# Row operands for the weight gradients: packed fp32 transposes in place of bf16 ones

## The chip, the cores and the metric

The kernel runs on one core of one Trainium2 chip. The metric is device time in microseconds of one execution. TensorE (PE) multiplies, VectorE (DVE) and ScalarE (ACT) work on tiles, GpSimd (POOL) does small copies and starts some of the DMA transfers, SyncE (SP) starts the others. Tiles lie in SBUF as 128 partitions by some number of elements; matmul results and transposes land in PSUM, of which the kernel uses eight banks of 128 x 512 fp32.

## The reference

Forward and backward of a speech encoder with a joint network, all tensors bf16. With B = 2, T = 16000, D = 256:

```
h  = gelu(conv(x, w1, 3 taps))[:, ::2]      # 8000 steps
f  = gelu(conv(h, w2, 3 taps))[:, ::2]      # 4000 steps
fe = f @ w_f;  ge = g @ w_g                 # ge: 8 rows
j  = tanh(fe[:, :, None] + ge[:, None])     # 4000 x 8
out = j @ w_o
# and, from grad_out (2, 4000, 8, 256), by the chain rule:
# the gradients of x, w1, w2, g, w_f, w_g and w_o
```

The gradients of w1, w2 and w_f are sums over time of outer products: for each tap, `dw[i] = sum over t of input[t + i]^T gradient[t]`. A matmul sums over partitions, so for these three gradients the inputs and gradients are needed with time in the partitions ("rows"), while all other work here holds the channels in the partitions.

## The kernel before

One unit of time is a quarter step q (4 steps of x, 2 of h, 1 of f). The 4000 steps of f of each batch are cut into 8 chunks of 512 (the last has 416), 16 chunks in all. Inside a chunk, `blocks` cuts 512 into four blocks of 128 steps (416 into 128, 128, 128, 32).

A chunk n goes through these stages, and each is a Python generator that yields after each small group of instructions:

- `conv_units`, `conv2_units`, `fe_units`: the forward pass (matmuls L241, L274, L297; gelu by helper L191), channels in partitions. Tile HT holds h as even and odd steps (`par` 0 and 1), FT holds f, G1 and G2 the gelu derivatives.
- `joint_units`, once per pair of the 8 rows u: matmul with w_o transposed (L518), the tanh derivative on DVE (L520), the output matmul (L574) and its copy on ACT (L576), the sum over u by an identity matmul (L531) into NGFE, and the gradient of w_o (`gwo`, L621), whose row operand JR is made by DMA transposes on SP's queue (L548).
- `d1_units`, `d5_units`: backward through w_f (L334, tile GF) and through w2 (L363, tile GH, even and odd steps). `d1_units` also issues the loads of x rows (`load_x5`): tile X5 holds, for each of 128 quarter steps, five steps of x in a row (4q-1 to 4q+3), 2560 bytes in one partition.
- `gw2_units`: the gradients of w2 and w_f. First it makes rows. For each block of 128 steps, eight 128x128 bf16 PE transposes (helper `transposes`, L374) go into one PSUM bank: HT even, HT odd, HT odd one step earlier, GF, each in two halves of 128 channels. One DVE copy of 128x1024 (L376) moves them to a tile of pool `rowp`. Then FT and NGFE are transposed, two blocks to a bank. Then come 8 matmuls of 256 columns for each of three taps (L416), and 8 for w_f (L425). Each sum stands in PSUM and is added by DVE to an fp32 accumulator in SBUF (`flush`, L317).
- `e_units`: transposes of GH (16 in two banks), the gradient of x (`gx_block`, L467, copied by ACT at L470, stored by POOL's queue at L479), and the gradient of w1 (`gw1`, L489, 16 matmuls of 256 columns per tap, rows of GH against X5).

So a chunk has 64 bf16 transposes and 8 copies L376 for these rows, and 80 matmuls of 256 columns that use them. Chunks of 511 or 417 steps arise in `e_units`, where the window of x is shifted by one step. The other transposes at L374, of JT, belong to `jr_block` and have no part in the change.

The order is written by the main loop: while chunk n's `joint_units` runs as `main`, `weave` takes units of a `fill` chain, in which the backward stages of chunk n-1 and the forward stages of chunk n+1 alternate (`islice(gw2, 6)` ends after the six groups of transposes, `islice(e, 5)` after two groups of transposes and three more units). The last chunk's backward stages run alone after the loop. Pools hand out tiles in a ring: `rowp` six, `x5p` four, PSUM `psp` five banks. A stage that asks for a tile of a ring waits until the last reader of the tile that it replaces is done.

POOL's queue carries, in order, the x row loads (L170, L173, L177), the stores of the x gradient (L479) and of the output (L605), and small copies. At the start POOL makes the identity and issues the loads of w1 (L642), g (L644) and w_g (L645).

Of the kernel before, what the change touches and what calls it, by code (L numbers as in the profile page):

```python
# [13 lines left out]
BF16 = mybir.dt.bfloat16  # L14
FP32 = mybir.dt.float32
# [6 lines left out]
P = 128  # L22
KT = 2
KK = 3
D = 256
# [6 lines left out]
def kernel(  # L32
# [22 lines left out]
    nc = tc.nc  # L55
    B, T, _ = x.shape
    MQ = T // 4
    NCH = (MQ + CW - 1) // CW
# [9 lines left out]
    def blocks(w):  # L68
        return [(o, min(P, w - o)) for o in range(0, w, P)]

    pool = lambda name, bufs, **kw: ctx.enter_context(tc.tile_pool(name=name, bufs=bufs, **kw))
    const = pool("const", 1)
    xcp = pool("xcp", 6)
# [6 lines left out]
    gfp = pool("gfp", 2)  # L80
    ghp = pool("ghp", 2)
    rowp = pool("rowp", 6)
    x5p = pool("x5p", 4)
    gxp = pool("gxp", 2)
    jtp = pool("jtp", 7)
    gotp = pool("gotp", 5)
# [10 lines left out]
    def ps_f32():  # L97
        return psp.tile([P, 512], FP32, name="ps", tag="ps")
# [3 lines left out]


    ident = const.tile([P, P], BF16, name="ident")
    W1 = const.tile([P, KK, KT, D], BF16, name="W1")
    W2 = const.tile([P, KK, KT, D], BF16, name="W2")
    WF = const.tile([P, KT, D], BF16, name="WF")
# [53 lines left out]
        return lo, hi  # L161

    def load_x5(n, o, M):
        pin = tc.keep_in_program_order
        b = chunks[n][0]
        q0 = window(n)[0] + o
        t = x5p.tile([P, 5, D], BF16, name="X5")
        if q0 == 0:
            nc.vector.memset(t[0:1, 0, :], 0.0)
            pin(nc.gpsimd.dma_start(out=t[0:1, 1:5, :], in_=x[b, 0:4, :].rearrange("(o f) d -> o f d", o=1)))  # L170
            src = x[b, 3:4, :]
            ap5 = bass.AP(tensor=src.tensor, offset=src.offset, ap=[[4 * D, M - 1], [1, 5 * D]])
            pin(nc.gpsimd.dma_start(out=t[1:M].rearrange("p f d -> p (f d)"), in_=ap5))  # L173
        else:
            src = x[b, 4 * q0 - 1:4 * q0, :]
            ap5 = bass.AP(tensor=src.tensor, offset=src.offset, ap=[[4 * D, M], [1, 5 * D]])
            pin(nc.gpsimd.dma_start(out=t[:M].rearrange("p f d -> p (f d)"), in_=ap5))  # L177
        S[n]["X5", o] = t

    def scratch(name, spare):  # L180
# [138 lines left out]
    def d1_units(n):  # L319
        b, ci, c0, W = geom(n)  # L320
        st = S[n]
        lo, hi = window(n)
        for (o, M) in blocks(hi - lo):
# [46 lines left out]
    def transposes(srcs, dsts):  # L370

        ps = ps_bf()
        for src, j, M in srcs:
            nc.tensor.transpose(out=ps[:M, j, :], in_=src, identity=ident[:])  # L374
        for dst, M, j0, j1 in dsts:
            nc.vector.tensor_copy(out=dst, in_=ps[:M, j0:j1, :])  # L376

    def gw2_units(n):
        b, ci, c0, W = geom(n)
        st = S[n]  # L380
        HT, GF, FT, NG = st["HT"], st["GF"], st["FT"], st["NGFE"]
        bl = blocks(W)
        HG = []
        for (o, M) in bl:
            t = rowp.tile([P, 8, P], BF16, name="rows")
            srcs = []
            j = 0
            for (par, off) in ((0, 2), (1, 2), (1, 1)):
                for kt in range(KT):
                    srcs.append((HT[:, par, kt, off + o:off + o + M], j, M))  # L390
                    j += 1
            for kt in range(KT):
                srcs.append((GF[:, kt, 2 + o:2 + o + M], j, M))
                j += 1
            transposes(srcs, [(t[:M], M, 0, 8)])
            HG.append(t)
            yield
        FN = []
        for k in range(0, len(bl), 2):
            t = rowp.tile([P, 8, P], BF16, name="rows")  # L400
            srcs, dsts = [], []
            for j, (o, M) in enumerate(bl[k:k + 2]):
                for kt in range(KT):
                    srcs.append((FT[:, kt, o:o + M], 4 * j + kt, M))
                    srcs.append((NG[:, kt, o:o + M], 4 * j + 2 + kt, M))
                dsts.append((t[:M, 4 * j:4 * j + 4, :], M, 4 * j, 4 * j + 4))
                FN.append((t, 4 * j, M))
            if all(M == P for _, M in bl[k:k + 2]):
                dsts = [(t[:, :, :], P, 0, 8)]
            transposes(srcs, dsts)  # L410
            yield
        for i, place in ((1, 0), (2, 2), (0, 4)):
            ps = ps_f32()
            for k, (o, M) in enumerate(bl):
                for dt in range(KT):
                    nc.tensor.matmul(ps[:, dt * D:(dt + 1) * D], lhsT=HG[k][:M, place + dt, :],  # L416
                                     rhs=HG[k][:M, 6:8, :].rearrange("p k d -> p (k d)"),
                                     start=(k == 0 and dt == 0), stop=(k == len(bl) - 1 and dt == KT - 1))
# [4 lines left out]
        for k, (t, j, M) in enumerate(FN):  # L423
            for dt in range(KT):
                nc.tensor.matmul(ps[:, dt * D:(dt + 1) * D], lhsT=t[:M, j + dt, :],  # L425
                                 rhs=t[:M, j + 2:j + 4, :].rearrange("p k d -> p (k d)"),
                                 start=(k == 0 and dt == 0), stop=(k == len(FN) - 1 and dt == KT - 1))
        flush("F", ACCF[:], ps[:])
        first_flush["F"] = False
        yield  # L430

    def e_units(n):
# [3 lines left out]
        N = hi - lo  # L436
        GH = st["GH"]
        bl = blocks(N)
        GR = []
        for k in range(0, len(bl), 2):  # L440
            t = rowp.tile([P, 8, P], BF16, name="rows")
            srcs, dsts = [], []
            for j, (o, M) in enumerate(bl[k:k + 2]):
                for par in range(2):
                    for kt in range(KT):
                        srcs.append((GH[:, par, kt, 2 + o:2 + o + M], 4 * j + 2 * par + kt, M))
                dsts.append((t[:M, 4 * j:4 * j + 4, :], M, 4 * j, 4 * j + 4))
                GR.append((t, 4 * j))
            if all(M == P for _, M in bl[k:k + 2]):
                dsts = [(t[:, :, :], P, 0, 8)]  # L450
            transposes(srcs, dsts)
            yield

        def gx_block(o, M):
# [27 lines left out]

        def gw1(i):
            ps = ps_f32()
            for k, (o, M) in enumerate(bl):
                t, j = GR[k]
                for dt in range(KT):
                    for par in range(2):
                        nc.tensor.matmul(ps[:, dt * D:(dt + 1) * D],  # L489
                                         lhsT=st["X5", o][:M, i + 2 * par, dt * P:(dt + 1) * P],  # L490
                                         rhs=t[:M, j + 2 * par:j + 2 * par + 2, :].rearrange("p k d -> p (k d)"),
                                         start=(k == 0 and dt == 0 and par == 0),
                                         stop=(k == len(bl) - 1 and dt == KT - 1 and par == 1))
            flush("1", ACC1[:, i, :], ps[:])

        for k, (o, M) in enumerate(bl):
# [332 lines left out]
```

## Time and profile before

| what | value |
|---|---|
| median of 3 runs | 951.14 us (947.83 to 953.77) |
| profiled execution | 953.21 us, of which 951.4 us from first to last instruction (the span) |
| PE busy | 914.8 us (96%), 6976 matmuls and transposes |
| DVE busy | 633.1 us (67%) |
| ACT busy | 614.4 us (65%) |
| POOL busy | 144.8 us (15%) |
| DMA queues, share of 16 engines | 64.3% (SP's queue) and 25.2% (POOL's queue) |
| mean granted TensorE clock | 0.989 |

A row's time in the profile is that of one instruction from its start to its modelled end. Matmuls overlap in the pipeline, so the distance between the starts of two neighbours is shorter than the duration of either, and that distance is what a matmul costs PE.

### The profile page before, as it was taken

To read this page: it belongs to the slowest core of one execution; us is meant where nothing else is said; L and a number is where in the kernel's file an instruction comes from. 1 tells how busy PE (TensorE), PEld (TensorE's weight loads), DVE (VectorE), ACT (ScalarE), POOL (GpSimd) and SP (SyncE) were. 2 spreads that over 40 slices of the span, in tenths; PEclk is the share of its full clock that TensorE was granted. 3 is DMA by queue.
4 is the path that set the end of the run, shared out by engine and by line. 5 is a ranking of instruction groups with operands and counts; after the bars stand their busy time and mean duration, and the time that the engine had idled before them with its cause. 6 is when DMAs were issued, how large, how long until landed. Compare 5 with 4: busy or idle time off the path is not lost.

```text
span 951.4 us, 18311 instructions
## 1 busy us (share of the span) xinstructions
PE 914.8 (96%) x6976; PEld 629.1 (66%) x6976; DVE 633.1 (67%) x1364; ACT 614.4 (65%) x972; POOL 144.8 (15%) x279
## 2 busy tenths in 40 slices
PE   7889998999999999999999999899999999999997
PEld 3455665767667576766756667576676757677775
DVE  5887847678494866748587494865939578494634
ACT  2878484765848567583865848568484866858433
POOL 1002121121111112021111202012021120202121
PEclk9989999999999999999999999999999999999999
DMA  9769999799998999898799999989989997897742
GB/s 189 175 125 221 194 207 204 198 230 186 212 196 206 206 203 244 183 219 187 156 211 192 200 206 209 198 190 221 205 208 228 188 226 179 191 215 183 198 132 87
DMA packets 381816, 185.69 MB, mean 195 GB/s; under 512 B 329904, under 2 KB 365512, under 8 KB 381728
## 3 DMA queue, kind: packets, MB, share of 16 engines
q1 hardware_dynamic: 362016, 114.35, 64.3%
q0 software_dynamic: 19712, 70.18, 25.2%
q8 instruction: 54, 0.88, 0.4%
q14 instruction: 34, 0.28, 0.1%
HBM read 54.43 MB, written 50.34 MB: 110 GB/s over the span
## 4 chain that ended last, share of the span: by engine, by line
PE 53%; DVE 24%; ACT 17%; DMA 4%; issue 2%; POOL 0%; SPq 0%; ACTq 0%; POOLq 0%; DVEq 0%
PE ps L489 8%; PE ps L467 7%; PE ps L574 7%; PE GWO_ps L621 6%; DVE g_sq L191 6%; DVE g_s L191 5%; ACT JT L307 5%; PE ps L518 5%; PE pst L374 5%; PE ps L274 4%; DVE NGZ L520 4%; DVE GH L366 4%; DMA JR<-JT 3%; ACT OUT L576 3%; PE NGps L531 2%; ACT JSQ L512 2%
## 5 line engine op out<-in xcount | busy, mean ns | idle before, releaser
L520 DVE SCALAR_TENSOR_TENSOR NGZ<-JSQ,ps 128x512 bf16<-128x512 bf16 (+1 forms) x256 | 167.7, 668 | 108.1 <-PE ps L518 102.9
L576 ACT CAST OUT<-ps 128x512 bf16<-128x512 f32 (+1 forms) x256 | 150.4, 591 | 81.7 <-PE ps L574 80.1
L307 ACT ACTIVATE JT<-FE,GE 128x512 bf16<-128x512 f32 (+1 forms) x256 | 172.8, 717 | 2.6 <-PE ps L574 2.0
L512 ACT ACTIVATE JSQ<-JT 128x1024 bf16<-128x1024 bf16 (+1 forms) x128 | 133.0, 1040 | 54.5 <-DVE NGZ L520 54.0
L621 PE MATMUL GWO_ps<-GO,JR 128*128 128x256 bf16 (+1 forms) x1024 | 153.1, 273 | 9.2 <-DMA JR<-JT 9.1
L574 PE MATMUL ps<-WO,JT 128*128 128x256 bf16 (+1 forms) x1024 | 156.0, 275 | 0.1
L518 PE MATMUL ps<-GOT,WOT 128*128 128x512 bf16 (+1 forms) x512 | 138.4, 374 | 6.3 <-DVE NGZ L520 5.9
L621 PEld LDWEIGHTS <-JR 128*128 128x128 bf16 (+1 forms) x1024 | 98.7, 97 | 50.2 <-DMA JR<-JT 14.0
L574 PEld LDWEIGHTS <-JT 128*128 128x128 bf16 (+1 forms) x1024 | 98.3, 99 | 32.1 <-issue 6.2
L317 DVE TENSOR_TENSOR ACC<-ACC,ps 128x512 f32<-128x512 f32 x90 | 61.4, 684 | 83.9 <-PE ps L489 80.4
L191 ACT ACTIVATE g_s<-g_s 128x1024 bf16<-128x1024 bf16 (+2 forms) x49 | 49.2, 1004 | 89.5 <-DVE g_s L191 89.5
L467 PE MATMUL ps<-W1T,GH 128*128 128x256 bf16 (+2 forms) x768 | 103.7, 272 | 0.0
L489 PE MATMUL ps<-rows,X 128*128 128x256 bf16 (+2 forms) x768 | 93.6, 272 | 0.0
L470 ACT CAST GX<-ps 128x512 bf16<-128x512 f32 (+2 forms) x128 | 75.3, 588 | 28.3 <-PE ps L467 19.4
L241 PE MATMUL ps<-XC,W 128*128 128x512 bf16 (+1 forms) x384 | 91.0, 374 | 0.7 <-DVE JR L376 0.5
L467 PEld LDWEIGHTS <-GH 128*128 128x128 bf16 (+2 forms) x768 | 74.7, 99 | 20.6 <-issue 1.6
L605 POOL DMA_DIRECT2D out_dram<-OUT x64 | 49.1, 767 | 247.5 <-ACT OUT L576 244.1
L376 DVE COPY rows<-pst 128x1024 bf16<-128x1024 bf16 (+5 forms) x134 | 85.8, 655 | 1.4 <-PE pst L374 1.4
L479 POOL DMA_DIRECT2D out_dram<-GX x64 | 35.3, 552 | 321.1 <-ACT GX L470 315.7
L489 PEld LDWEIGHTS <-X 128*128 128x128 bf16 (+2 forms) x768 | 73.7, 97 | 14.8 <-issue 3.0
L531 PE MATMUL NGps<-NGZ,ident 128*128 128x512 bf16 (+1 forms) x256 | 80.3, 374 | 0.1
L191 DVE TENSOR_TENSOR g_sq<-g_x 128x1024 bf16<-128x1024 bf16 (+2 forms) x49 | 32.1, 655 | 68.1 <-ACT g_x L244 39.3
(122 smaller groups left out, 1156.7 us busy)
## 6 DMA issues: line engine op xcount, KB each, us to landing
GO<-in_grad_out_dram SPq DMA_DIRECT2D x56, 512.0 KB, 4.2
out_dram<-OUT POOLq DMA_DIRECT2D x56, 512.0 KB, 4.8
X<-in_x_dram POOLq DMA_DIRECT2D x58, 320.0 KB, 7.6
out_dram<-GX POOLq DMA_DIRECT2D x58, 256.0 KB, 3.0
JR<-JT SPq DMA_TRANSPOSE x240, 3.7
GO<-in_grad_out_dram SPq DMA_DIRECT2D x8, 384.0 KB, 3.9
out_dram<-OUT POOLq DMA_DIRECT2D x8, 384.0 KB, 4.1
GOT<-in_grad_out_dram SPq DMA_TRANSPOSE x128, 4.9
```

What stands on the lines that cost most here:

```text
L191: later.popleft()()
L241: nc.tensor.matmul(ps[:, :W], lhsT=W1[:, i, kt, mt * P:(mt + 1) * P], rhs=st["X", c][:, kt, 16 + sh:16 + sh + W], start=(k == 0), stop=(k ...
L307: nc.scalar.activation(out=JT[:, mt, :W], in_=S[n]["FE"][:, mt, :W], func=ACT.Tanh, bias=GE[:, b, mt, u:u + 1], scale=1.0)
L467: nc.tensor.matmul(ps[:Mx, cj * D:(cj + 1) * D], lhsT=GH[:, par, kt, j:j + Mx], rhs=W1T[:, i, kt, :], start=(k == 0), stop=(k == last))
L489: nc.tensor.matmul(ps[:, dt * D:(dt + 1) * D], lhsT=st["X5", o][:M, i + 2 * par, dt * P:(dt + 1) * P], rhs=t[:M, j + 2 * par:j + 2 * par + ...
L512: nc.scalar.activation(out=JSQ[:, :, :W], in_=JT[:, :, :W], func=ACT.Square)
L518: nc.tensor.matmul(ps[:, :W], lhsT=WOT[:, kt, mt * P:(mt + 1) * P], rhs=GOT[:, kt, :W], start=(kt == 0), stop=(kt == KT - 1))
L520: nc.vector.scalar_tensor_tensor(out=NGZ[:, mt, :W], in0=JSQ[:, mt, :W], scalar=1.0, in1=ps[:, :W], op0=ALU.subtract, op1=ALU.mult, accum_ ...
L531: nc.tensor.matmul(st["NGps"][:, mt, :W], lhsT=ident[:], rhs=st["NGZ", u][:, mt, :W], start=(u == 0), stop=(u == U - 1))
L574: nc.tensor.matmul(ps[:M, j * V:(j + 1) * V], lhsT=st["JT", u][:, kt, o:o + M], rhs=WO[:, kt, :], start=(kt == 0), stop=(kt == KT - 1))
L576: nc.scalar.copy(out=OUT[:M, k, :], in_=ps[:M, :])
L621: nc.tensor.matmul(GWO_ps[:, dt, :], lhsT=JR[:M, k, j, dt, :], rhs=GO[:M, k, j * V:(j + 1) * V], start=(n_gwo[0] == 0), stop=(n_gwo[0] == ...
```

## The change

Two neighbouring steps of a bf16 tile, four bytes, are seen as one fp32 number, and PE transposes 128 channels by 128 such numbers with an fp32 identity. One transpose then gives rows for 256 steps: partition p holds steps 2p and 2p+1 of each channel, next to each other (`r` = 0, 1). `pairs` cuts a chunk into blocks of 256 steps, two steps per partition, and the x rows are loaded in the same layout (X5 has two groups of five steps in a partition; `x5p` has two tiles of twice the size). The row copy on DVE moves the same bits as bf16. Each matmul of the weight gradients takes one `r`: its operands read every second bf16 element of a row tile. The rows of HT odd one step earlier are needed only for r = 0 (for r = 1 the rows of HT odd, r = 0, are the same numbers), and they are made by two bf16 transposes whose source takes every second step.

```
+    ident32 = const.tile([P, P], FP32, name="ident32")
...
     def load_x5(n, o, M):
+        t = x5p.tile([P, 2, 5, D], BF16, name="X5")
+        def load(p0, p1, r0, r1, f0):
+            src = x[b, 4 * (q0 + 2 * p0 + r0) - 1 + f0:4 * (q0 + 2 * p0 + r0) + f0, :]
+            ap = bass.AP(tensor=src.tensor, offset=src.offset,
+                         ap=[[8 * D, p1 - p0], [4 * D, r1 - r0], [1, (5 - f0) * D]])
+            dst = t[p0:p1, r0:r1, f0:5, :].rearrange("p r f d -> p r (f d)")
+            tc.keep_in_program_order(nc.gpsimd.dma_start(out=dst, in_=ap))
...
-        if ci == NCH - 1:
+        if ci == NCH - 1 or N % 2 == 1:
             nc.gpsimd.memset(GH[:, :, :, 2 + N:3 + N], 0.0)
...
+    def packed_rows(srcs, M, shifted=()):
+        t = rowp.tile([P, 4, P, 2], BF16, name="rows")
+        ps = ps_f32()
+        for j, src in enumerate(srcs):
+            nc.tensor.transpose(out=ps[:M, j * P:(j + 1) * P], in_=src.bitcast(FP32), identity=ident32[:])
+        n4 = 2 * P * len(srcs)
+        flat = ps[:].bitcast(BF16)
+        for j, src in enumerate(shifted):
+            nc.tensor.transpose(out=flat[:M, n4 + j * P:n4 + (j + 1) * P], in_=src, identity=ident[:])
+        n4 += P * len(shifted)
+        nc.vector.tensor_copy(out=t[:M].rearrange("p k d r -> p (k d r)")[:, 0:n4], in_=flat[:M, 0:n4])
+        return t
...
     def gw2_units(n):
+        bl = pairs(W)
+        for (o, M) in bl:
+            HR.append(packed_rows([HT[:, par, kt, 2 + o:2 + o + 2 * M] for par in range(2) for kt in range(KT)], M))
+            yield
+            GR.append(packed_rows([GF[:, kt, 2 + o:2 + o + 2 * M] for kt in range(KT)], M,
+                                  [HT[:, 1, kt, 1 + o:1 + o + 2 * M:2] for kt in range(KT)]))
+            yield
+        for (o, M) in bl:
+            FN.append(packed_rows([t[:, kt, o:o + 2 * M] for t in (FT, NG) for kt in range(KT)], M))
+            yield
...
+                        nc.tensor.matmul(ps[:, dt * D:(dt + 1) * D], lhsT=lhsT, rhs=GR[k][:M, 0:2, :, r],
+                                         start=(j == 0), stop=(j == last))
...
     def e_units(n):
+        for (o, M) in bp:
+            GR.append(packed_rows([GH[:, par, kt, 2 + o:2 + o + 2 * M] for par in range(2) for kt in range(KT)], M))
             yield
...
+                            nc.tensor.matmul(ps[:, dt * D:(dt + 1) * D],
+                                             lhsT=st["X5", o][:M, r, i + 2 * par, dt * P:(dt + 1) * P],
+                                             rhs=GR[k][:M, 2 * par:2 * par + 2, :, r],
+                                             start=(j == 0), stop=(j == last))
...
     make_identity(nc, ident[:])
+    nc.gpsimd.tensor_copy(out=ident32[:], in_=ident[:])
```

In the built program a chunk has 28 fp32 and 4 bf16 transposes for these rows in place of 64 bf16 ones, 8 row copies as before (two of them of 768 elements instead of 1024), and the same 80 matmuls of 256 columns. Each fp32 transpose is one load of 128 columns of weights and one matmul of 128 columns. The x rows take 38 DMA issues on POOL instead of 66, for the same bytes.

More of the change, by code (lines that the diff above doesn't have):

```diff
@@ L69, in blocks, with pairs @@
         return [(o, min(P, w - o)) for o in range(0, w, P)]
+    def pairs(w):
+        return [(o, min(P, (w - o + 1) // 2)) for o in range(0, w, 2 * P)]
     pool = lambda name, bufs, **kw: ctx.enter_context(tc.tile_pool(name=name, bufs=bufs, **kw))
@@ L82 @@
     rowp = pool("rowp", 6)
-    x5p = pool("x5p", 4)
+    x5p = pool("x5p", 2)
     gxp = pool("gxp", 2)
@@ L163, in load_x5 @@
     def load_x5(n, o, M):
-        pin = tc.keep_in_program_order
         b = chunks[n][0]
         q0 = window(n)[0] + o
-        t = x5p.tile([P, 5, D], BF16, name="X5")
-        if q0 == 0:
[L169 to L177, printed above, removed]
+        t = x5p.tile([P, 2, 5, D], BF16, name="X5")
[5 more added lines that the diff above has]
+            tc.keep_in_program_order(nc.gpsimd.dma_start(out=dst, in_=ap))
+        p0, p1 = 0, M
+        if q0 == 0:
+            nc.vector.memset(t[0:1, 0, 0, :], 0.0)
+            load(0, 1, 0, 1, 1)
+            load(0, 1, 1, 2, 0)
+            p0 = 1
+        if q0 + 2 * M > MQ:
+            base = (M - 1) // 32 * 32
+            nc.vector.memset(t[base:M, 1, :, :], 0.0)
+            p1 = M - 1
+            load(M - 1, M, 0, 1, 0)
+        load(p0, p1, 0, 2, 0)
         S[n]["X5", o] = t
@@ L322, in d1_units @@
         lo, hi = window(n)
-        for (o, M) in blocks(hi - lo):
+        for (o, M) in pairs(hi - lo):
             load_x5(n, o, M)
@@ L381, in gw2_units @@
         HT, GF, FT, NG = st["HT"], st["GF"], st["FT"], st["NGFE"]
-        bl = blocks(W)
-        HG = []
+        bl = pairs(W)
+        HR, GR = [], []
         for (o, M) in bl:
[L385 to L396, printed above, removed]
+            HR.append(packed_rows([HT[:, par, kt, 2 + o:2 + o + 2 * M] for par in range(2) for kt in range(KT)], M))
+            yield
+            GR.append(packed_rows([GF[:, kt, 2 + o:2 + o + 2 * M] for kt in range(KT)], M,
+                                  [HT[:, 1, kt, 1 + o:1 + o + 2 * M:2] for kt in range(KT)]))
@@ L397, in gw2_units @@
             yield
         FN = []
[L399 to L410, printed above, removed]
+        for (o, M) in bl:
+            FN.append(packed_rows([t[:, kt, o:o + 2 * M] for t in (FT, NG) for kt in range(KT)], M))
@@ L411, in gw2_units @@
             yield
-        for i, place in ((1, 0), (2, 2), (0, 4)):
+        for i in (1, 2, 0):
             ps = ps_f32()
+            last = 4 * len(bl) - 1
+            j = 0
             for k, (o, M) in enumerate(bl):
[L415 to L418, printed above, removed]
+                flat = GR[k][:M].rearrange("p k d r -> p (k d r)")
+                for r in range(2):
+                    for dt in range(KT):
+                        if i == 1:
+                            lhsT = HR[k][:M, dt, :, r]
+                        elif i == 2:
+                            lhsT = HR[k][:M, 2 + dt, :, r]
+                        elif r == 1:
+                            lhsT = HR[k][:M, 2 + dt, :, 0]
+                        else:
+                            lhsT = flat[:, 4 * P + dt * P:4 * P + (dt + 1) * P]
+                        nc.tensor.matmul(ps[:, dt * D:(dt + 1) * D], lhsT=lhsT, rhs=GR[k][:M, 0:2, :, r],
+                                         start=(j == 0), stop=(j == last))
+                        j += 1
@@ L422, in gw2_units @@
         ps = ps_f32()
[L423 to L427, printed above, removed]
+        j, last = 0, 4 * len(bl) - 1
+        for k, (o, M) in enumerate(bl):
+            for r in range(2):
+                for dt in range(KT):
+                    nc.tensor.matmul(ps[:, dt * D:(dt + 1) * D], lhsT=FN[k][:M, dt, :, r], rhs=FN[k][:M, 2:4, :, r],
+                                     start=(j == 0), stop=(j == last))
+                    j += 1
         flush("F", ACCF[:], ps[:])
@@ L438, in e_units @@
         bl = blocks(N)
+        bp = pairs(N)
         GR = []
[L440 to L451, printed above, removed]
+        for (o, M) in bp:
+            GR.append(packed_rows([GH[:, par, kt, 2 + o:2 + o + 2 * M] for par in range(2) for kt in range(KT)], M))
             yield
@@ L484, in gw1 @@
             ps = ps_f32()
[L485 to L493, printed above, removed]
+            j, last = 0, 8 * len(bp) - 1
+            for k, (o, M) in enumerate(bp):
+                for r in range(2):
+                    for dt in range(KT):
+                        for par in range(2):
+                            nc.tensor.matmul(ps[:, dt * D:(dt + 1) * D],
+                                             lhsT=st["X5", o][:M, r, i + 2 * par, dt * P:(dt + 1) * P],
+                                             rhs=GR[k][:M, 2 * par:2 * par + 2, :, r],
+                                             start=(j == 0), stop=(j == last))
+                            j += 1
             flush("1", ACC1[:, i, :], ps[:])
```

## The prediction

> **What bounds the kernel now.** First the page's busy row and its slices.
>
> ```profile
> span 951.4 us, 18311 instructions
> ...
> PE 914.8 (96%) x6976; PEld 629.1 (66%) x6976; DVE 633.1 (67%) x1364; ACT 614.4 (65%) x972; POOL 144.8 (15%) x279
> ...
> PE   7889998999999999999999999899999999999997
> ```
>
> PE is busy in nearly every slice between start and tail, the others two thirds. A busy PE may still be a slow one, so I read the distance between starts in the timeline of PE, where FT and NGFE are turned into rows, and further on GH:
>
> ```profile
> 97.01 0.60 PE L574 MATMUL ps<-WO,JT 128*128 128x256 bf16 x4
> 97.45 0.27 PE L621 MATMUL GWO_ps<-GO,JR 128*128 128x256 bf16 x1
> 97.56 0.38 PE L531 MATMUL NGps<-NGZ,ident 128*128 128x512 bf16 x1
> 97.77 0.22 PE L374 MATMUL pst<-ident,FT 128*128 128x128 bf16 x1
> 97.83 0.22 PE L374 MATMUL pst<-ident,NGFE 128*128 128x128 bf16 x1
> 97.88 0.22 PE L374 MATMUL pst<-ident,FT 128*128 128x128 bf16 x1
> ...
> 98.16 0.22 PE L374 MATMUL pst<-ident,NGFE 128*128 128x128 bf16 x1
> ...
> 111.98 0.62 PE L374 MATMUL pst<-ident,GH 128*128 128x128 bf16 x8
> ```
>
> (Columns: start in us, time, engine, line, operands, shape, count.) From 97.77 to 98.16 eight transposes start, one every 56 ns, although one lasts 0.22 us: the pipeline is full and the weight loads hide. The 512-column matmul ahead holds PE for 0.21 us (97.56 to 97.77), four of 256 columns for 0.44 us (97.01 to 97.45), 109 ns each. So PE passes one column per 0.42 ns, whatever runs. What is left is idle time: in the loop and over PE's waits,
>
> ```profile
> 60.00:915.00 855.00, 832.80 (x6402) 580.33 (x6402) 572.69 (x1211) 567.40 (x896) 132.47 (x250) 0.99 0.92 200
> ```
>
> ```profile
> PE GWO_ps L621 <- DMA JR<-JT: 9.1, 11, 1.9
> PE ps L518 <- DVE NGZ L520: 5.9, 10, 0.6
> ```
>
> The first shows 855 us of loop with PE busy 832.8 (then weight loads, DVE, ACT, POOL, clock, DMA share 0.92, GB/s), the second what PE waits for (us in total, times, longest). Only 22 us of the loop are not PE's. The kernel is bound by PE's columns, and PE time added or removed in the loop is time of the kernel, nearly one for one.
>
> **The change, part by part.**
>
> *Transposes.* Removed are 16 chunks x 64 = 1024 at 56 ns, 57.3 us. Added are 64 bf16 ones (3.6 us) and 448 fp32 ones at an unknown T: the change is 448 T - 53.8 us. It breaks even at T = 120 ns. No fp32 operand on PE is in this trace, so T is bounded from both sides. From below: 128 columns take 56 ns here, no less. From above: a weight load and a matmul after one another without overlap, by the longest rows, 139 + 219 = 358 ns:
>
> ```profile
> L374 PE MATMUL pst<-ident,GF 128*128 128x128 bf16 x124 | 17.0, 219 | 0.0
> ...
> L467 PEld LDWEIGHTS <-GH 128*127 128x127 bf16 x24 | 2.7, 138 | 0.0
> ...
> L374 PEld LDWEIGHTS <-GH 128*127 128x127 bf16 x8 | 0.6, 139 | 0.0
> ...
> L376 DVE COPY rows<-pst 128x1024 bf16<-128x1024 bf16 x120 | 80.4, 680 | 1.4 <-PE pst L374 1.4
> ```
>
> These rows also give the value that I take. Loads of 128 columns last 97 ns, loads of 127 columns 138: an odd count is read column by column (127 columns at 0.42 ns are 53 ns; 138 - 97 = 41). Yet the group at 111.98, whose last four transposes have such loads, takes 0.62 us for eight, where eight ordinary ones take 0.61: a slow load costs some 3 ns, because it still runs behind the matmul ahead. The built fp32 transpose is one such load and one 128-column matmul, so the nearest row says **T = 59 ns**, and 448 x 59 - 53.8 = **-27.3 us**. Ends kept: 56 ns (-28.7 us) and 358 ns (+106.6 us).
>
> The Trainium skill, "TensorE: Matmul & The Clock Gate", section Terms, says that the transpose mode is four times faster for fp32 than fp32 otherwise is. By that rule an fp32 transpose runs at the pace of bf16 columns, and the sum would be the one above; no run here shows it yet.
>
> *The 80 matmuls per chunk.* Their number and columns stay: 1280 in all (L489, L416, L425), 109 ns each, 139.5 us. Their moving operand, and for 448 of them the weights too, now read every second element. No row here steps that way. Lower end: no change, since the trace's operands that start at an odd element (sources shifted by one step at L241 and L363) keep 216 ns per 512 columns. Upper end: two elements fetched for each used, half pace, +139.5 us. I take nothing, by the shifted rows; slower weight loads have cover too, as six L467 matmuls with loads of 138 ns ran at 109 ns each.
>
> The Trainium skill, "SBUF — State Buffer", Specifications, says that SBUF is read in lines of 16 bytes and that two hits per line give full rate. By that rule a step of 4 bytes is free; no row here shows it.
>
> *DVE.* Row copies stay at 8 per chunk; 32 of them shrink from 1024 to 768 elements. Between the rows of 512 elements (411 ns) and 1024 (680 ns) that is 545, so 32 x 0.13 = 4.3 us less on an engine 67% busy: nothing on the path in the loop. Two memsets of 32 partitions x 1280 are added, each about the 0.5 us of the start's 128x528 memset, hidden likewise; uncovered they would cost 1 us.
>
> *POOL and DMA.* 28 of 66 issues of 0.54 us go, 15 us of an engine 15% busy: nothing. The bytes are the same. Two larger X5 tiles come free with the same last `gw1` matmul as four did, so the loads start as before; they land in 7.6 us and are first used 38 us after issue (77.4 to 115.4), and a load twice as long stays under that. Without this cover it would be some 8 us per chunk. Behind these loads in POOL's queue stand only the stores. The identity's fp32 copy stands ahead of the load of w_g, whose landing is on the chain of the start: +0.3 us, like the 0.32 us select beside it.
>
> *Waits.* The fp32 transpose's weight load now carries the wait for the PSUM bank as well as that for data, so at the head of a group of four it can't be loaded ahead while the bank is taken. Behind it stands all of PE's queue. Price where it bites: the load's 139 ns; PE waits of that kind at L374 are 1.7 us in all here, so I put 1 us.
>
> *Sum.* 15 chunks in the loop: 15 x 1.71 = -25.6 us. In the last chunk, alone after the loop, seven row copies fill DVE without a gap while PE ends early, so there only about 0.5 us. Given back: PE reaches JR's transposes earlier while DMA is at 0.92 of its engines, and 9.1 us of waits for JR grow by an estimated 2. -25.6 - 0.5 + 2 + 1 + 0.3 = **-22.8 us**: the span 951.4 becomes 928.6, the profiled execution 953.2 about 930.4. The median, 951.1, lies 2 us under the profiled execution, within the runs' spread, so **928 us** is the forecast.
>
> **Rivals.**
>
> *A 4-byte column counts as two.* If PE takes 4 bytes at half pace, or the 32-bit weights fill both of the places that let a load run ahead (load 53 + matmul 56), T = 109: 448 x 109 - 53.8 = -5.0 us, **946 us**, within noise. For it: the array has only been seen with 2-byte operands here. Against: nothing in the trace.
>
> *Four passes, slower than before.* If PE runs an fp32 transpose internally as four passes of 56 ns, T = 224, +46.6 us: **about 998 us**. It decides from T = 120 ns, and costs over 1% from 141. For it: fp32 on PE is unseen here. Against: one load and one matmul in the program.
>
> The Trainium skill, "FP8 and Floating Point Precision", TensorE Precision Notes, says that true fp32 takes four passes; by that rule this rival holds. It speaks of multiplying, and no run here shows which rule covers a transpose.
>
> *No overlap.* If the load of 32-bit weights waits until the matmul ahead has streamed, T = 139 + 56 = 195, +33.6 us: **985 us**. Against it is the group at 111.98, with 2-byte weights.
>
> *Half pace for strided operands.* All 1280 matmuls at 218 ns: +139.5 - 27.3, **about 1063 us**. Part of it, weights alone, hides.
>
> *The time doesn't follow PE.* PE gets 27 us shorter and waits for JR, or DVE in the gelu stages, take it back: **940 to 951 us**. Against: DVE at 572.7 of 855 us, DMA at 0.92.
>
> **How the numbers follow.** Forecast (922 to 936 us) 0.48; two columns 0.20 (942 to 951); given back 0.06; no overlap 0.10 (up to 985); four passes or worse, up to T = 358, 0.10 (998 to 1058); strided operands 0.06. A measurement of this kernel can tell about 1% from no change. Faster by over 1% (under 941.6): 0.48 + a part of those given back = 0.50; within 1%: 0.24; slower: 0.26. Range: 922 to 986 leaves out four passes and strided operands, 0.16; the forecast's own range is 922 to 936.
>
> **What the profile after would show.** Right: fp32 transposes 59 ns apart with loads near 139 ns, the 256-column matmuls of the weight gradients 109 ns apart as before, PE busy some 25 us lower with its share still over 94%, waits for JR little over 9 us. T near 109 or 224 shows in the same timeline; strided cost shows as L489's successors over 109 ns. The forecast is wrong if any of these distances is larger, or if PE's idle time in the loop grows from 22 us by more than 10.

## The result and the profile after

The changed kernel takes **1039.9 us** (median, 1035.8 to 1041.7) where the kernel before, run beside it, takes 949.9: a ratio of **1.094**, 95% interval 1.089 to 1.099. The forecast was 928, the range 922 to 986. So the time rose by some 90 us where a fall of 23 was expected, and it lies outside the range.

The page of the changed kernel, its span, busy row, slices of PE and granted clock:

```profile
span 1034.0 us, 17258 instructions
...
PE 921.7 (89%) x6464; PEld 630.3 (61%) x6464; DVE 631.4 (61%) x1360; ACT 613.4 (59%) x972; POOL 142.4 (14%) x254
...
PE   6987299898999989999989918979899899999998
...
PEclk9999599999999989999999968989999999999999
```

The span grew by 82.6 us (951.4 to 1034.0), and PE's busy time by only 6.9 (914.8 to 921.7). The rest, 75.7 us, is PE standing idle. Two holes show in PE's slices, a 2 in the fifth and a 1 in the 24th, and the clock falls in the same places.

PE's waits of the changed kernel (us in total, times, longest):

```profile
PE GWO_ps L639 <- DMA JR<-JT: 81.0, 19, 24.9
...
PE ps L692 <- DMA WG<-in_w_g_dram: 2.7, 1, 2.7
...
PE pst L686 <- DMA GR<-in_g_dram: 1.5, 1, 1.5
```

The first was 9.1 us in 11 waits before: **+71.9 us**. The other two, at the start, were 0.4 in all: +3.8. With the 6.9 of busy time that makes the 82.6; of the other rows of PE's waits the largest, for NGFE (L349), went from 0.8 to 4.7 us, and all the others together changed less. So nearly all of the loss is a wait for the row operand JR of the w_o gradient, in which the change has no part. Its waits are of two kinds: one of 24.9 us in the first chunk of each batch (ends at 123.59 and 624.75 us), and 31 us in 17 shorter ones, up to 5.7 us, in most other chunks.

**The long ones.** DMA issues of x rows, after and then before (count, size of each, median us from issue to landing):

```profile
X<-in_x_dram POOLq DMA_DIRECT2D x28, 640.0 KB, 9.1
...
X<-in_x_dram POOLq DMA_DIRECT2D x2, 635.0 KB, 35.1
```

```profile
X<-in_x_dram POOLq DMA_DIRECT2D x58, 320.0 KB, 7.6
...
X<-in_x_dram POOLq DMA_DIRECT2D x4, 317.5 KB, 7.7
```

Loads of 640 KB land in 9.1 us. The first block of a batch has no row at step -1, so it loads 127 partitions, two rows each; it is less than a per cent smaller and takes 35.1 us. Its packets show how: 127 large ones follow one another, one every 0.20 to 0.25 us from 84 to 116 us, with 1905 (15 x 127) packets of 8 bytes beside them. X itself is in time. What is late is everything else. SyncE's queue in the changed kernel (start, time, what it issues):

```profile
82.86 1.28 SPq L146 DMA_TRANSPOSE GOT<-in_grad_out_dram  x1
84.19 1.58 SPq L154 DMA_DIRECT2D GO<-in_grad_out_dram  x1
85.86 21.28 SPq L146 DMA_TRANSPOSE GOT<-in_grad_out_dram  x1
107.23 7.72 SPq L136 DMA_TRANSPOSE XC<-in_x_dram  x1
115.04 5.78 SPq L140 DMA_TRANSPOSE XC<-in_x_dram  x3
120.93 5.54 SPq L566 DMA_TRANSPOSE JR<-JT  x4
```

One transpose is held for 21.28 us where another one just ahead took 1.28; behind it XC, behind that JR, and PE idles from 98.7 to 123.6 us.

**The short ones.** PE in the second chunk of the loop (a time in brackets is idle time before the row, with what ended it):

```profile
181.26 0.71 PE L639 MATMUL GWO_ps<-GO,JR 128*128 128x256 bf16 x5
184.92 0.28 PE L639 MATMUL GWO_ps<-GO,JR 128*128 128x256 bf16 x1 [2.94 <-DMA JR<-JT]
...
186.57 0.63 PE L399 MATMUL ps<-ident,FT 128*128 128x128 f32 x2
187.00 0.64 PE L399 MATMUL ps<-ident,NGFE 128*128 128x128 f32 x2
```

The matmul at 184.92 that needs the new JR stands ahead of the FT and NGFE transposes. In the kernel before, at the same point of its second chunk, it stands behind them (at 159.43):

```profile
155.64 0.22 PE L374 MATMUL pst<-ident,FT 128*128 128x128 bf16 x1
...
156.53 0.22 PE L374 MATMUL pst<-ident,NGFE 128*128 128x128 bf16 x1
...
157.24 0.27 PE L621 MATMUL GWO_ps<-GO,JR 128*128 128x256 bf16 x1
159.43 0.36 PE L621 MATMUL GWO_ps<-GO,JR 128*128 128x256 bf16 x1 [1.92 <-DMA JR<-JT]
```

No matmul of PE's queue ran ahead of the one that waited, so the 2.94 us hold up the transposes that stand behind it. And the wait costs more than itself. Stretches of the changed kernel (PE, PEld, DVE, ACT, POOL busy, then the granted clock, DMA share, GB/s):

```profile
182.00:185.00 3.00, 0.08 (x1) 0.09 (x2) 3.00 (x8) 0.05 (x1) 0.00 (x0) 1.00 0.82 176
...
186.00:189.00 3.00, 3.00 (x15) 2.48 (x14) 1.90 (x4) 1.54 (x2) 0.20 (x1) 0.50 0.56 94
189.00:192.00 3.00, 3.00 (x19) 1.73 (x18) 0.21 (x1) 1.38 (x3) 0.00 (x0) 0.99 1.08 293
```

For 3 us after the wait the clock is 0.50: two FT transposes take 0.43 us where they take 0.21 at full clock. The Trainium skill, "TensorE: Matmul & The Clock Gate", section "What's actually happening", says that the clock falls to half after an idle window of about 3.4 us and that these windows run freely and are not reset when a kernel starts. The trace agrees in kind: its half-clock stretches between start and tail last 3.41 us or a whole multiple of that. But less than a whole window of idle time was enough: 2.94 us here and 1.92 us in the kernel before (at 157.5), while 2.55 us (at 242.7 in the changed kernel) left the clock at 1.00. Of PE's busy time, 40.8 us lie at clock 0.50 in the changed kernel and 15.2 in the kernel before.

### The profile page after: what moved, and what is told of

Same layout as the page of the kernel before. It is cut to its first block, busy times and chain, and to the rows that moved or that the text cites. A ratio compares the mean times of both kernels' runs of the same rounds, so it can differ in the third digit from the quotient of the medians.

```text
span 1034.0 us, 17258 instructions
## 1 busy us (share of the span) xinstructions
PE 921.7 (89%) x6464; PEld 630.3 (61%) x6464; DVE 631.4 (61%) x1360; ACT 613.4 (59%) x972; POOL 142.4 (14%) x254
## 4 chain that ended last, share of the span: by engine, by line
PE 52%; ACT 21%; DVE 12%; SPq 5%; DMA 5%; issue 5%; POOL 0%; ACTq 0%; POOLq 0%; DVEq 0%
ACT JT L322 8%; PE ps L592 7%; PE GWO_ps L639 6%; PE ps L536 5%; PE ps L399 5%; PE ps L484 5%; PE ps L507 5%; DMA JR<-JT 4%; PE ps L440 4%; PE ps L289 4%; PE ps L256 3%; DVE g_sq L206 3%; DVE g_s L206 3%; ACT JSQ L530 3%; ACT GX L487 3%
## 5 line engine op out<-in xcount | busy, mean ns | idle before, releaser
L639 PE MATMUL GWO_ps<-GO,JR 128*128 128x256 bf16 (+1 forms) x1024 | 159.0, 275 | 81.0 <-DMA JR<-JT 81.0
L322 ACT ACTIVATE JT<-FE,GE 128x512 bf16<-128x512 f32 (+1 forms) x256 | 176.6, 729 | 2.3 <-PE ps L592 1.7
L592 PE MATMUL ps<-WO,JT 128*128 128x256 bf16 (+1 forms) x1024 | 160.6, 280 | 0.0
L405 DVE COPY rows<-ps 128x1024 bf16<-128x1024 bf16 (+3 forms) x128 | 82.7, 655 | 62.3 <-PE ps L403 51.0
L592 PEld LDWEIGHTS <-JT 128*128 128x128 bf16 (+1 forms) x1024 | 101.2, 100 | 31.5 <-issue 3.6
L206 ACT ACTIVATE g_s<-g_s 128x1024 bf16<-128x1024 bf16 (+2 forms) x49 | 49.2, 1004 | 89.0 <-DVE g_s L206 88.9
L507 PE MATMUL ps<-rows,X 128*128 128x256 bf16 (+1 forms) x768 | 96.2, 275 | 0.0
L549 PE MATMUL NGps<-NGZ,ident 128*128 128x512 bf16 (+1 forms) x256 | 84.2, 384 | 0.1
L507 PEld LDWEIGHTS <-X 128*128 128x128 bf16 (+1 forms) x768 | 73.7, 96 | 17.1
```

What stands on the lines that cost most here:

```text
L206: later.popleft()()
L322: nc.scalar.activation(out=JT[:, mt, :W], in_=S[n]["FE"][:, mt, :W], func=ACT.Tanh, bias=GE[:, b, mt, u:u + 1], scale=1.0)
L507: nc.tensor.matmul(ps[:, dt * D:(dt + 1) * D], lhsT=st["X5", o][:M, r, i + 2 * par, dt * P:(dt + 1) * P], rhs=GR[k][:M, 2 * par:2 * par + ...
L592: nc.tensor.matmul(ps[:M, j * V:(j + 1) * V], lhsT=st["JT", u][:, kt, o:o + M], rhs=WO[:, kt, :], start=(kt == 0), stop=(kt == KT - 1))
L639: nc.tensor.matmul(GWO_ps[:, dt, :], lhsT=JR[:M, k, j, dt, :], rhs=GO[:M, k, j * V:(j + 1) * V], start=(n_gwo[0] == 0), stop=(n_gwo[0] == ...
```

## The experiments

Ratios are to the kernel before, run on the same chip in the same series. "JR" is PE's wait for JR in the profiled execution.

| run | what it is | us | ratio (95%) | JR, us |
|---|---|---|---|---|
| changed | | 1039.9 | 1.094 (1.089 to 1.099) | 81.0 |
| e1 | changed, the 127-partition load split | 1004.3 | 1.050 (1.047 to 1.054) | 46.4 |
| e2 | changed, all x row loads split | 999.3 | 1.047 (1.042 to 1.052) | 45.3 |
| e3 | before, with the changed loads alone | 1005.6 | 1.051 (1.044 to 1.058) | 62.2 |
| e4 | e2 with bf16 transposes | 970.7 | 1.017 (1.015 to 1.019) | 28.7 |
| e5 | before, matmul pinned | 949.5 | 1.001 (0.9995 to 1.003) | 0 |
| e6 | before, XC late | 966.6 | 1.018 (1.014 to 1.023) | 0 |
| e7 | e4, XC late | 959.4 | 1.011 (1.008 to 1.015) | 4.7 |
| e8 | e2, XC late | 941.6 | 0.993 (0.991 to 0.996) | 2.5 |
| e9 | changed, matmul pinned | 990.8 | 1.043 (1.037 to 1.049) | 35.7 |
| e10 | e2, matmul pinned | 948.6 | 0.996 (0.992 to 0.999) | 0 |
| e11 | e4, matmul pinned | 940.9 | 0.990 (0.988 to 0.993) | 0 |
| e12 | changed, pinned, load cut 126+1, 112+15 | 949.0 | one run | 0 |
| e13 | changed, pinned, load cut 113+14, 125+2 | 966.5 | one run | 16.2 |
| e14 | changed, pinned, nine rows | 948.7 | 0.996 (0.993 to 0.998) | 0 |
| e15 | e14 with bf16 transposes | 940.2 | 0.986 (0.983 to 0.990) | 0 |

### The form of the load, and the parts one by one

e1 loads the 127 partitions in two pieces of one row each; e2 does so with every load.

```
-        load(p0, p1, 0, 2, 0)
+        load(p0, p1, 0, 1, 0)       # e1: only where p0 is 1
+        load(p0, p1, 1, 2, 0)
```

e3 is the kernel before with `load_x5` and `pairs` of the changed one, and for the gradient of w1 rows by bf16 transposes of every second step. e4 is e2 with this form everywhere:

```
+        for r in range(2):
+            for j, src in enumerate(srcs):
+                nc.tensor.transpose(out=ps[:M, r * k + j, :], in_=src[:, r::2], identity=ident[:])
...
+                            lhsT = HR[k][:M, 4 * r + dt, :]
```

> The changed kernel, except that the x rows of a batch's first block (127 partitions of two rows each) are loaded in two transfers of one row per partition. Same bytes, same work on every engine. Theory A (the two waits of 24.9 us for JR, one in each batch's first chunk, come from that one form of transfer, which takes 35 us and holds up the DMA transposes on SP's queue): both waits go, PE's waits for JR fall from 81 us to about 31, the time from 1040 to about 990. Rival B (the stall comes from the row layout or from the amount loaded at that point, not from the form of this transfer): a wait of over 15 us stays at both places and the time stays above 1025.

> The changed kernel with every x row load cut in two transfers of one row per partition (320 KB each, as in the kernel before). Theory A1 (the other 31 us of waits for JR come from transfers of 640 KB, which keep the DMA engines from the transposes twice as long as 320 KB ones): waits for JR fall to about the 9 us of the kernel before, time about 968. Rival A2 (those waits come from something else, such as stages on PE that moved): 25 us or more of the waits stay, and the time is that of the run with only the first block split, about 990.

> The kernel before with the loads of the changed kernel alone: x rows two steps per partition, and for the gradient of w1 the same number of bf16 transposes as before, whose source takes every second step, so that all matmul operands stay contiguous. No fp32 transposes, no strided matmul operands. Theory A (the loads make most of the loss): waits for JR of 70 to 85 us with two of about 25 us, time 1010 to 1030. Rival C (fp32 transposes and strided operands make the loss, the waits are a follow-up of a slower PE): time 950 to 960.

> The run with every load cut in two, with each fp32 transpose replaced by two bf16 transposes whose sources take every second step, rows written to the tile one step after the other, so that all matmul operands are contiguous. 60 bf16 transposes per chunk instead of 28 fp32 and 4 bf16. By the distances in the trace of the changed kernel (fp32 transposes 109 ns and up to 164 to 187 in the groups of FT and NGFE, strided matmuls 113 instead of 109 ns) the fp32 transposes and strided operands cost about 12 us more than this: 955 if the run with split loads is at 968. If fp32 pairs are worth having, this run is slower than that one.

*Measured.* In e1 both long waits are gone (5.4 and 3.9 us are left in their places) and the time is 35.6 us lower; JR waits fell by 34.6. On SyncE's queue the GOT transpose that was held for 21.28 us now takes 4.66:

```profile
87.98 4.66 SPq L146 DMA_TRANSPOSE GOT<-in_grad_out_dram  x1
```

All JR waits, though, are 46.4 us where 31 had been expected, and the time is 1004 in place of 990: the short waits of the other chunks grew too, from 31 to 37 us, and why was not followed up. The waits of e1 and of e3:

```profile
PE GWO_ps L643 <- DMA JR<-JT: 46.4, 18, 6.1
```

```profile
PE GWO_ps L631 <- DMA JR<-JT: 62.2, 16, 22.4
```

e3 has the long waits back (21.8 and 22.4 us) with no packed transpose in it, and is 51 us slower than the kernel before. So the form of this one load makes the long waits, as theory A said in both; its sizes for e3 were too high (70 to 85 us of waits and 1010 to 1030 us, measured 62.2 and 1005.6). e2 refutes A1: with 320 KB loads the short waits stay (45.3 us against 46.4), so the size of the loads does not make them. Yet e3, with 640 KB loads, has only three short waits over 1.2 us where e1 has eleven: they come with something that e3 leaves as it was. e4 was faster than e2 by 28.5 us, more than the 12 expected; 16.6 us of that are JR waits, so the two differ by more than PE's price.

What e3 leaves as it was is the order of PE's queue. The build's scheduler places instructions elsewhere than the written order does, and I counted PE's columns in the built queues (at 0.42 ns, fp32 transposes twice) from the chunk's first matmul on NGFE to the first matmul that needs the new JR: 21.4 us in the kernel before and in e3, 19.6 in e4, 18.7 in the changed kernel, e1 and e2. JR waits, without the two long ones, rise as the place moves ahead: 9.1 and 18, then 28.7, then 31 to 46. The order fits; one place has waits of different size, so the place is not all that sets them. (The expectations of the next two groups give 17.9 and, pinned, 29.7 for the changed kernel; there each group of fp32 transposes had been counted once. Rightly counted they are 18.7 and 31.5.)

### The place of the w_o gradient's matmul, and XC

e5 is the kernel before with that matmul tied to its written place, e6 to e8 issue XC for the chunk after next behind JR on SyncE's queue:

```
+                if j == 0 and dt == 0 and k == 0:
+                    tc.keep_in_program_order(mm)
```

```
-            if up == 2 and n + 2 < G:
-                load_x(n + 2)
...
                 load_jr(*orderp[step + 1])
+            if up == 2 and n + 2 < G:
+                load_x(n + 2, tc.keep_in_program_order)
```

> The kernel before, with one thing changed: the first matmul of each block row of the w_o gradient is pinned to its written place in PE's queue instead of the later place that the build's scheduler gives it. In the built order, counted in PE's work since the chunk's first matmul on NGFE, the matmul that needs JR (whose DMA transposes stand behind those of XC in SP's queue) then stands at 17.4 us instead of 21.4, ahead of the FT and NGFE transposes. No instruction is added or removed and no DMA changes. Theory A (the 2 to 6 us waits for JR in each chunk of the changed kernels arise since this matmul stands earlier in PE's queue, at 17.9 in the changed kernel and 19.6 in the run with bf16 transposes, while JR lands 23 to 25 us after the loads of x rows): waits for JR of 9 us grow to 40 to 60 us, time 985 to 1000. Rival B (those waits come from the x row loads or the row transposes, the place does not matter): waits stay near 9 us and the time under 960.

> The kernel before, with the four transposes of XC for the chunk after next issued on SP behind the row transposes JR of the next pair instead of ahead of the one that PE waits for; PE's order is unchanged. Theory A: the 9 us of waits for JR fall under 4 us, time 943 to 951. Rival B (XC becomes late for the conv, or JR is late for another reason): waits of 9 us or more for JR or XC, time 951 or more.

> The run with bf16 transposes and split loads, with XC issued behind JR as in the run beside it. PE's order is unchanged, so the matmul that needs JR still stands at 19.6 us. Theory A (its 28.7 us of waits for JR come from JR landing later than this place): waits under 8 us, time 946 to 954, level with the kernel before. Rival B (two steps per partition make the x row loads slower and with them all DMA): 20 us or more of the waits stay, time 965 to 971.

> The changed kernel with all loads split and XC issued behind JR. Theory A: waits for JR fall from 45 us to under 12, time about 965. What then remains over the run with bf16 transposes beside it is PE's own price for fp32 transposes and strided operands: by the busy time of PE (928.8 against 912.7 us) about 16 us. Rival B (PE's price is only the 5 to 7 us that follow from 109 ns per fp32 transpose plus 5 us of strided matmuls): 10 to 12 us over the run beside it.

*Measured.* The forecast for e5 fell, by a misreading of mine: the matmul that I had found at 17.4 us belongs to the pair before. The one that needs the new JR stands at 31.2 us in the pinned queue, so its written place is *later*, and it is the scheduler that moves it ahead of its place. Read so, e5 agrees with theory A: JR waits went from 9.1 us to none. The time stayed (1.001): other waits filled in, the longest row being

```profile
PE ps L334 <- ACT NGFE L535: 11.7, 14, 0.9
```

against 0.8 us before. In e8 JR lands earlier instead, and its waits fall from 45.3 to 2.5 us, the time from 999 to 942: under the 965 expected, and faster than the kernel before. That fp32 version had been 28.5 us behind its bf16 twin; now it is ahead of it, so the 16 us that I had read from PE's busy time were for the most part no price of fp32 columns. They were half-clock time after waits: 55.8 us of PE's busy time lie at clock 0.50 in e2 and 26.0 in e4, and half of the difference is 14.9 us. e6 and e7 have almost no JR waits on PE left, as expected, but e6 is slower than the kernel before and e7 misses its 946 to 954: XC late makes JR of another pair late, and ACT waits before it may write a new JT, 33.3 us in e6 and 38.1 in e7, against 6.3 in e8 and no such wait before. Why e8 escapes was not followed up. Moving XC is no clean remedy, and e7 against e8 no clean price; pinning gives both.

### Both remedies, and the price of the packed form

e9 pins the matmul in the changed kernel alone, e10 in e2, e11 in e4. e12 cuts the 127 partitions by partitions:

```
+            cut = 1 + (126 if b == 0 else 112)
+            load(p0, cut, 0, 2, 0)
+        load(cut, p1, 0, 2, 0)
```

> The changed kernel with one thing changed: the first matmul of each block row of the w_o gradient is pinned to its written place in PE's queue, which is later (29.7 us of PE's work after the chunk's first matmul on NGFE) than the place that the scheduler gives it (17.9 us). Loads, fp32 transposes and strided operands stay. Theory A (place in PE's queue and the two slow loads make the loss together): the waits of 2 to 6 us in the other chunks go; the two stalls shrink from 24.9 us by the 10 to 12 us that PE now has other work for; time 955 to 975. Rival B (fp32 transposes and strided operands themselves cost the 28 us that separate the two runs with split loads): 1010 or more.

> The changed kernel with every x row load cut in two and with the pinned place of the w_o gradient's matmul. Theory A: waits for JR under 5 us, time 936 to 946, level with the run with split loads and XC issued late (941.6). Rival B (the fp32 transposes are slow on PE): 960 or more.

> As the run beside it, with each fp32 transpose replaced by two bf16 ones of strided sources and contiguous matmul operands. If PE's columns set the time once JR comes in time, this is the price of the packed form: 28 fp32 transposes of 122 ns mean distance, 4 bf16 ones and 80 strided matmuls of 4 ns more are 3.96 us per chunk against 3.36 us for 60 bf16 ones, so 9 us less than the run beside it: 927 to 937. Rival (something other than PE's columns sets the pace of a chunk): within 4 us of it, or slower.

> The changed kernel with the pinned place, and the first block's load of 127 partitions by two rows cut by partitions: 126 and 1 in the first batch, 112 and 15 in the second. Read from the landing times. Theory A (a load whose partition count is a multiple of 16 is spread over the DMA engines, another goes to one engine at 0.25 us per partition): 126 partitions take about 32 us, 112 under 9, 15 about 4 plus the start. Rival B (only an odd count is slow): 126 partitions take under 10 us.

*Measured.* e10 has no wait for JR left and takes 948.6 us, 91.4 less than the changed kernel (and a little above its 936 to 946). The two causes add up: pinning alone takes off 49.2 (e9), splitting all loads alone 40.7 (e2), 89.8 in all. In e9 the two long waits shrank by some 10 us each, as expected, to 15.4 and 15.0, but the time, 990.8, lies above the 955 to 975: JR waits of 35.7 us remain, 30.3 of them these two, and PE's busy time is 907.1 against 899.8 in e10 for the same instructions.

PE of e10 in the same part of a chunk:

```profile
155.86 0.38 PE L400 MATMUL ps<-ident,FT 128*128 128x128 f32 x2
156.07 0.38 PE L400 MATMUL ps<-ident,NGFE 128*128 128x128 f32 x2
156.37 0.44 PE L400 MATMUL ps<-ident,FT 128*128 128x128 f32 x2
156.64 0.38 PE L400 MATMUL ps<-ident,NGFE 128*128 128x128 f32 x2
156.86 0.60 PE L593 MATMUL ps<-WO,JT 128*128 128x256 bf16 x4
...
160.99 1.98 PE L441 MATMUL ps<-rows 128*128 128x256 bf16 x16
162.81 1.02 PE L537 MATMUL ps<-GOT,WOT 128*128 128x512 bf16 x4
...
167.81 0.60 PE L640 MATMUL GWO_ps<-GO,JR 128*128 128x256 bf16 x4
```

and the same transposes in e11:

```profile
210.45 0.27 PE L400 MATMUL pst<-ident,FT 128*128 128x128 bf16 x2
210.56 0.27 PE L400 MATMUL pst<-ident,NGFE 128*128 128x128 bf16 x2
210.67 0.28 PE L400 MATMUL pst<-ident,FT 128*128 128x128 bf16 x2
```

The matmul for the new JR now runs at 167.81, twelve us behind the FT transposes, with no idle time ahead. Two fp32 transposes take 0.21 us, two bf16 ones 0.11. Sixteen strided matmuls take 1.82 us (160.99 to 162.81), 114 ns each. Between starts the fp32 transposes of e10 are mostly 109 ns apart; the first of a group often costs 164, and the mean is 120. A bf16 matmul right behind one also starts 109 ns later (all 36 of 512 columns in the loop), though its own weights are bf16: the time goes with the fp32 transpose itself and not with a load behind it. So 448 of them cost 53.8 us, as much as the net 960 bf16 ones took. The packed transposes give PE nothing, and the strided operands (1280 x 4 ns) cost it 5 us. Against e11, with 60 bf16 transposes per chunk, I expected 9 us; measured are **7.7** (948.6 and 940.9; for e11 itself 927 to 937 had been expected).

e12's cuts were all quick: 126 partitions in 6.9 us, 112 in 6.3, 15 in 5.9. Theory A, which gave 126 some 32 us, fell: a multiple of 16 is not needed, and 15 shows that an odd count is not slow as such. e12 changes only the first load of each batch and leaves the others whole, and its one run takes 949.0 us, level with e10.

### What form is slow, and nine rows

> The changed kernel with the pinned place, the first block's load cut in 113 and 14 partitions in the first batch and 125 and 2 in the second, two rows each. Theory A (a count above 16 that has no divisor, like 127, makes the slow form): 113 partitions take about 28 us, with some 1700 packets of 8 bytes, and PE waits for JR of over 8 us in the first batch's first chunk; 125 take under 9. Rival B (only odd counts are slow): both take about 30 us. Rival C (127 alone): both take under 9 us.

> The changed kernel with the pinned place and the x rows as nine rows in a row per partition (steps 8p-1 to 8p+7, 4608 bytes) in place of two times five with one row loaded twice: one contiguous piece per partition, a tenth less bytes, and no partition-by-row form. Theory A (with JR in time, the loads are off the path): waits for JR under 5 us and the time that of the run with split loads and the pinned place, 944 to 950. Rival B (the loads' bytes still count): 938 or less.

> The same nine rows and pinned place with two bf16 transposes of strided sources for each fp32 one and contiguous operands. Theory A: as the run with bf16 transposes, split loads and the pinned place, 937 to 944, faster than the kernel before by about 1%, and 6 to 9 us under the run beside it. Rival B: over 946.

e14 takes the nine steps 8p-1 to 8p+7 as one piece per partition; e15 does so in e11:

```
+        t = x5p.tile([P, 9, D], BF16, name="X5")
+            ap = bass.AP(tensor=src.tensor, offset=src.offset, ap=[[8 * D, p1 - p0], [1, (f1 - f0) * D]])
...
+                                             lhsT=st["X5", o][:M, 4 * r + i + 2 * par, dt * P:(dt + 1) * P],
```

DMA issues of x rows in e13:

```profile
X<-in_x_dram POOLq DMA_DIRECT2D x1, 625.0 KB, 10.8
X<-in_x_dram POOLq DMA_DIRECT2D x1, 565.0 KB, 33.2
...
X<-in_x_dram POOLq DMA_DIRECT2D x1, 70.0 KB, 30.0
```

*Measured.* 113 partitions by two rows take 33.2 us with 1697 packets of 8 bytes, and the 14 partitions issued behind them 30.0; PE waits 13.3 us for JR in that batch's first chunk. 125 take 10.8 us, more than the 9 expected, and 126, in e12, 6.9. So among loads of two rows per partition the slow ones are those whose count has no divisor from 2 to 16, as theory A said; 125, with none but 5, is in between.

The Trainium skill, "DMA: Bandwidth & Descriptors", section "Why a DMA increments its semaphore by 16 and not by 1", gives the rule: a transfer runs on the largest number of engines up to 16 that divides the size of its outermost dimension on both sides, and names 127 partitions as running on one. By it 113 and 127 get one engine, 125 five, 126 fourteen, 112 sixteen. The landing times agree, in this order: 33.2 and 35.1, 10.8, 6.9, 6.3 us; which engine carried a packet the trace does not tell. The page also names an exception, by which some direct copies started by POOL are spread over up to 16 engines whatever their count, 127 partitions over all 16; 127 partitions by *one* row would be such a one here, at 7.7 us in the kernel before and, as one piece of 4608 bytes each, 7.0 in e14.

e14 is level with e10 (948.7 and 948.6), so a tenth less bytes buys nothing once JR is in time. e15 repeats the price of the packed form, 8.5 us, and at 940.2 us is as fast as e11: both beat the kernel before by about 1%. With e15, of about 11 us gained over the kernel before, 64 fewer transposes explain 3.6. The rest was not traced.

## Why the prediction was wrong

- **What bounds the kernel.** Right for the kernel before: PE's columns, with 22 us of idle time in the loop. It didn't carry over. I read "DMA share 0.92" and 9.1 us of waits for JR as a term of 2 us, while JR in the kernel before lands at nearly the moment that PE asks for it, in most chunks (11 waits, the longest 1.9 us). The place of one matmul in PE's queue kept that, and the changed queue moved it 2.7 us ahead (21.4 to 18.7). PE's idle time in the loop went from 22 to 95 us, where a growth of more than 10 was to show that the forecast is wrong.
- **POOL and DMA: "nothing".** This is the step that failed most. Its cover was that x rows land in 7.6 us and are used 38 us after issue, "and a load twice as long stays under that". The load took 35.1 us, and its own user was indeed not late. The step looked for who waits for this load, and behind it in POOL's queue; those held up were the DMA transposes of another queue, and behind them JR. Measured by e1: 35.6 us; with the matmul pinned, by e9 against e10: 42.2.
- **Given back for JR: 2 us.** Measured: 71.9 us of JR waits in all, of which about 50 are the two long ones and 22 are more and longer short ones. Pinning the matmul takes 49.2 us off the changed kernel, half-clock time included.
- **Transposes, T = 59 ns.** Wrong by one of the rivals named: "a 4-byte column counts as two", T = 109, forecast at 0.20. The distance is 109 ns with a mean of 120, and 448 x 120 - 53.8 is 0 in place of -27.3. The nearest row, slow weight loads of 127 columns, was the wrong analogy: it bounds the load, and what takes twice as long is the column. The rule that I had cited from the Trainium skill's page "TensorE: Matmul & The Clock Gate", section Terms ("4× faster for FP32"), as I read it, would have made the fp32 transpose run at bf16's pace; the trace shows half of it. Four passes (T = 224) did not hold either.
- **Strided operands: nothing.** 113 to 114 ns instead of 109: 1280 x 4 = 5 us in place of 0. By the rule of two hits per 16-byte line in the Trainium skill, "SBUF — State Buffer", Specifications, it would be free; measured it costs 4%, far from half pace.
- **Start: +0.3 us** for the identity's copy ahead of the load of w_g. The waits there are 3.8 us longer, 1.5 of them for the load of g, which is issued ahead of the copy, so the copy can't explain these. In the runs without this copy (e3, e4, e11, e15) the wait for w_g is 0.3; with it 1.4 to 2.7, but 0.4 in e8. How much of it the copy makes is open.
- **DVE and the added waits: nothing and +1.** DVE's busy time fell from 633.1 to 631.4 us and no row shows PE waiting for the row copies longer than before; the first term held, and nothing speaks against the second.
- **The rivals.** Those that made the kernel slower were all costs of PE. That 1039.9 lies within the band of "four passes or worse" (998 to 1058) is chance: T was 120, and the time came from waits. "The time doesn't follow PE" did name waits for JR, but let them take back no more than PE gained; no rival had a load whose form changes.

The terms, from 928.6 to 1034.0 of span: transposes +27.3, strided operands +5, JR +70, start +3.5, together 105.8 for 105.4. The time at half clock, which sits in PE's busy time, is not among them: 40.8 us against 15.2 before, at half pace, would add some 13. So it is luck that the sum closes so nearly; something of that size, not found here, stands against it.

## What to carry to other kernels

Look at the shape of every transfer that a change creates, its odd first and last blocks above all: a partition count with no divisor from 2 to 16 can make the whole load several times slower, and other transfers pay, not the load's own user. When a scheduler orders the queue, compare where the instructions that wait for DMA stand before and after: a change of some transposes moved one such matmul 2.7 us ahead and cost tens of us. And read PE's busy time beside the granted clock: 28 us between two variants shrank to 8 when neither waited.

## What the runs showed of the hardware

- A load of 127 or 113 partitions by two rows takes 35.1 or 33.2 us, with 15 packets of 8 bytes per partition; 126 take 6.9. While the one of 127 runs, a DMA transpose on another queue, which takes 4.7 us with the load split, is held for 21.
- fp32 transposes of 128 x 128 start 109 ns apart at full clock, twice the 56 of bf16, and so move the same bytes in the same time.
- bf16 matmul operands that take every second element cost 113 to 114 ns per 256 columns instead of 109.
- After an idle time of 2.94 us the granted clock was 0.50 for 3.4 us, after one of 1.92 too, after one of 2.55 not. Once nothing waited for JR (e10), the loop from 60 to 915 us ran at a mean clock of 1.00.
